# Capped attention and a top-1 expert layer in one kernel: two row steps, an eviction and a rank step change places

## The chip, the cores and the metric

One core of a Trainium2 chip runs the kernel. The time is device microseconds of one execution; the kernel before took 529.63 us, the median of three runs (528.35 to 530.30). Smaller is better. TensorE (PE) multiplies and transposes, VectorE (DVE), ScalarE (ACT) and GpSimd (POOL) work element by element, and SyncE (SP) issues most of the DMAs, one after the other in the order of its queue.

## What is computed

Attention over 4 batches, 12 heads, 448 positions of 64, with a tanh cap on the scores; its output is the input of a mixture of 8 experts, each token going to the one expert with the largest logit.

```python
scores = cap * np.tanh(scale * np.matmul(q, k.transpose(0, 1, 3, 2)) / cap)
attn = np.exp(scores - scores.max(-1, keepdims=True))
attn = attn / (attn.sum(-1, keepdims=True) + 1e-09)
x = np.matmul(attn, v).transpose(0, 2, 1, 3).reshape(1792, 768)
logits = x @ w_gate                      # 8 experts
e_idx = np.argmax(logits, axis=1)
gate_w = softmax(logits)[arange, e_idx]
eom = sigmoid(x @ w_output_gate)         # 8 columns
h = np.maximum(x[mask] @ w1[e], 0.0)     # for each expert e; mask = (e_idx == e)
out[mask] = gate_w[mask, None] * eom[mask, e, None] * (h @ w2[e])
```

## The kernel before

Attention runs in 24 units: unit u is one pair of heads of one batch, six units to a batch (batches 0 to 3). In unit u TensorE forms four blocks of scores (`qk(u, 0..3)`), ScalarE takes tanh and exp of each, and TensorE multiplies the exponentials of unit u - 1 with V (`pv(u - 1, ...)`) into one PSUM bank. `u_evac(u - 1)` (L335) then copies that bank to an SBUF tile `ut` of seven buffers: from unit 18 on ScalarE does it, except for unit 22; VectorE does it for the others. `presum(u, ...)` adds up the exponentials for the denominators, on GpSimd up to unit 21 and on VectorE for units 22 and 23. `prep(u + 2)` turns and splits K and Q of the unit after the next (tiles tk, tq).

Around these the program hangs small steps in numbered slots, by hand. Slot x of the table `at` (L507) of batch 2 is met in unit 19 + x // 4, at the place x % 4 of that unit: 0 ahead of the first pv matmuls, 1 behind them, 2 behind the third block of scores, 2.5 behind `u_evac`, 3 at the end. A batch's steps are the gate matmuls and logits, `choose` (the expert of each token), `rank_mm` and `place` (the token's place within its expert), `enter` (which scatters index and weight of each token to the tables `tab` in DRAM, four GpSimd DMAs), and six row steps `rws[0..5]`: `row_tr` (L478) turns the ut of one pair by four transposes into PSUM (tile trow), `row_out` (L485) scales it on VectorE (tile xr, four buffers) and sends it to the rows `xs` in DRAM, on SyncE's queue, for batch 3 on GpSimd's. In attention trow shares the two PSUM buffers of tag "t" with tk, tq and the rank's tile trk. `RWP` (L53) holds the slots of rows 1 to 5, row 0 has its own; `NXP` puts the six steps of `early()` into slot 7: small VectorE operations that plan the first five blocks of tokens and write the plan, `meta`. Slot 10.5 puts on SyncE's queue the table fetches of the first two blocks (`fetch_dma`, tc<-tab, four DMAs each, whose addresses come from meta) and the first weight chunk; slots 15 and 16 put the first two `gather` on GpSimd's queue and the other weight chunks on SyncE's. `gather(i)` reads the tokens' rows from xs (batches 0 to 2) into xg, and so waits for all their rows.

The experts follow: blocks of 128 tokens, each weight chunk split by ScalarE (high part) and VectorE (low part) into planes, up to six ahead, then matmuls in two sweeps (`mm1`, `mm2`). The first two blocks share their planes (`two1`, `two2`). The steps of batch 3 are the list `bg`, which `STEPS` (L58) spells out: one word to a step, one letter to a part (r rank_mm, p place, q positions, e enter, a digit a row step, n the next part of the later plan `late()`). The first two steps stand ahead of `two1`, the next twelve behind its twelve chunks, two behind the last chunks of block 2, the rest in `two2`. There a row is turned into the tile of tag "hph", which has one buffer.

Of the kernel before, what the change touches and what calls it, by code (L numbers as in the profile page):

```python
# [21 lines left out]
def tile_kernel(ctx: ExitStack, tc, q, k, v, cap, w_gate, w_ogate, w1, w2, out):  # L22
    nc = tc.nc
    B, H, S, D = q.shape
# [5 lines left out]
    NU = B * NP  # L30
# [19 lines left out]
        COL.update({k: NW + i * NO + j for j, k in enumerate(k for k in OWN if KIND[k] == kind)})  # L50
    AH = 6
    PZ = 4
    RWP = (9, 10, 12, 13, 14)  # L53
    NXP = (7, 7, 7, 7, 7, 7)
    F1 = 5
    F2 = 4
    PRE = 3
    STEPS = 'g s S G x0 X1 l2 c rp3 n4 n5 q e n n n n n n zh'  # L58
    WARM = (32, 8, 12, 0)
    RB = 7  # L60
    SP0 = 3
# [2 lines left out]
    UACT = 18  # L64
# [269 lines left out]

    def u_evac(u):  # L335
        t = utp.tile([128, S], F32, tag="ut", name="ut")
        if UACT <= u < NU - 2 or u == NU - 1:
            nc.scalar.activation(out=t, in_=ups.pop(u), func=ACTF.Copy)  # L338
        else:
            nc.vector.tensor_copy(out=t, in_=ups.pop(u))  # L340
        ut[u] = t
# [22 lines left out]
    def end_of_batch(b):  # L364
# [130 lines left out]
        rws = [L(P(row_tr, p), P(row_out, p)) for p in range(NP)]  # L495
        t = [sums_out, L(sums_tr, recips), L(P(gate_mm, 0), P(gate_out, 0)), L(P(gate_mm, 1), P(gate_out, 1))]
        gts = [L(P(gate_tr, g), P(gate_mul, g)) for g in range(2)]
        if b < B - 2:
            at = {1: [t[2], t[3]], 2: [sums_out], 5: [t[1]], 6: [rws[0]], 9: [gts[0]], 10: [rws[1]], 13: [gts[1]], 14: [rws[2]],
                  15: [logits], 16: [choose], 18: [rws[3]], 21: [rank_mm, place], 22: [rws[4]], 23: [place2], 24: [enter]}  # L500
            at.setdefault(26 if b < B - 3 else 22, []).append(rws[5])
        elif b == B - 2:
            g = early()
            nx = P(next, g, None)
            lds = [P(load_raw, 0, w, c) for w in range(2) for c in range((KD, KF)[w])]
            fd = [P(fetch_dma, i) for i in range(NE)]
            at = {-1: [sums_out], 1: [t[2], t[3]], 2: [t[1], *gts], 3: [logits], 4: [choose],  # L507
                  6: [rws[0]], 6.5: [rank_mm, place, place2, enter]}
            for i, x in enumerate(RWP, 1):
                at.setdefault(x, []).append(rws[i])  # L510
            for i, x in enumerate(NXP):
                at.setdefault(x, []).append(nx)
            for x, fs in ((10.5, [fd[0], fd[1], P(set_known, NE), lds[0]]), (15, [P(gather, 0), *lds[1:6], fd[2]]),
                          (16, [P(gather, 1), fd[3], *lds[6:]])):
                at.setdefault(x, []).extend(fs)
        if b < B - 1:
            for x, fs in at.items():
                for f in fs:
# [4 lines left out]
                  e=enter, n=nx, z=L(P(set_known, NSLOT), P(fetch_dma, NE)), h=lambda: next(rests(), None))  # L523
        do.update({str(p): rws[p] for p in range(NP)})
        return [L(*[do[x] for x in w]) for w in STEPS.split()]

# [60 lines left out]
    def early():  # L587


        cnt, key, srt, gt = M("cnt", [1, E]), M("key", [1, E]), M("srt", [1, E]), M("le", [1, E, E])  # L590
        cm, nb, nbp, more = M("cm", [1, E]), M("nb", [1, E]), M("nbp", [1, E]), M("more", [1, E])
        g14 = M("g14", [1, E, 14])
        lo, hi = M("lo", [1, 1, E]), M("hi", [1, 1, E])
        tt(cnt, pres[(B - 1) % 2][0:1, 0], ereg, ALU.subtract)

        stt(srt, cnt, float(E), ALU.mult, e8, ALU.subtract)
        ts(cm, cnt, -127.0, ALU.add)
        tt(gt, over(srt, E), srt.unsqueeze(2).to_broadcast([1, E, E]), ALU.is_gt)
        tt(g14, cm.unsqueeze(2).to_broadcast([1, E, 14]), mrow.unsqueeze(1).to_broadcast([1, E, 14]), ALU.is_gt)
        red(key, gt)  # L600
        red(nb, g14)
        yield

        ts(nbp, key, 0.0, ALU.is_equal, 2.0, ALU.mult)
        ts(more, key, float(E - 1), ALU.is_equal, float(NE), ALU.mult)
        tt(nbp, nbp, nb, ALU.max)
        tt(gt, over(key, E), key.unsqueeze(2).to_broadcast([1, E, E]), ALU.is_le)
        tt(nbp, nbp, more, ALU.add)
        yield
        tt(gt, gt, over(nbp, E), ALU.mult)  # L610
        red(hi[:, 0], gt)
        tt(lo[:, 0], hi[:, 0], nbp, ALU.subtract)
        yield
        yield from slots_of(lo, hi, nb, ereg.unsqueeze(1), 0, NE)
# [60 lines left out]
    def rests():  # L675

        full, h, hx, wo = rt["rest"]
        sh = [1, 2, NO, E]
        oh, o2 = M("roh", sh), M("ro2", sh)
        two = lambda x: x.unsqueeze(2).to_broadcast(sh)  # L680
        own = lambda i: metah[:, i, NW:].rearrange("a (z n) -> a z n", z=2)
        tt(wo, wo, over(full, NW), ALU.mult)
        tt(oh, two(hx), irow[:, 0:NO].unsqueeze(1).unsqueeze(3).to_broadcast(sh), ALU.is_equal)
        red(metah[:, 2, 0:NW], wo, ALU.max)
        tt(oh, oh, two(h), ALU.mult)
        tt(o2, oh, full.unsqueeze(1).unsqueeze(1).to_broadcast(sh), ALU.mult)
        red(own(1), oh, ALU.max)
        red(own(2), o2, ALU.max)
        tt(o2, oh, e8.unsqueeze(1).unsqueeze(1).to_broadcast(sh), ALU.mult)
        red(own(0), o2, ALU.max)  # L690
        yield
# [134 lines left out]
    for b in range(B - 1):  # L826
        end_of_batch(b)
# [32 lines left out]
    for u in range(NU):  # L860
# [24 lines left out]
        if u > 0:  # L885
            pv(u - 1, 3)
            u_evac(u - 1)
# [8 lines left out]
    u = NU - 1  # L896
# [245 lines left out]

    split_to(SP0)
    bg.extend(end_of_batch(B - 1))
    pv(u, NK)
    u_evac(u)
    tx(0)
    step()
# [96 lines left out]
```

## Time and profile before

| | |
|---|---|
| runs | 528.35, 529.63, 530.30 us |
| profiled execution | 529.51 us, of which the span is 527.9 us |
| busy: TensorE, VectorE, ScalarE, GpSimd | 97%, 65%, 73%, 56% of the span |
| mean granted clock of TensorE | 0.992 |

The span runs from the first to the last instruction; the remainder of the time lies around it. The shares are means over very unlike stretches: attention up to about 211 us, the experts from about 217 us. A wait counts for the end only where TensorE, or what follows it, has nothing else to do.

### The profile page before, as it was taken

The numbers are of one execution on the slowest core, as the hardware profiler recorded it, in microseconds if no ns is written. First come the engines' busy times: TensorE is split into PE (matmuls) and PEld (weight loads), VectorE is DVE, ScalarE is ACT, GpSimd is POOL, SyncE is SP. The second block draws the span as 40 slices with busy tenths as digits, with TensorE's granted clock in tenths as the row PEclk, the third lists the DMA queues.
The fourth block names the chain that finished last, engine by engine and source line by source line (L and its number), as shares of the span: only waits on it lengthen the run. The fifth ranks groups of instructions, "written<-read, shape, count | busy, mean of one in ns | idle before, by whom it ended". The sixth has DMA issues, their size and how long they took to land. (4 is left out here: it accounts for less than half of the span.)

```text
span 527.9 us, 10345 instructions
## 1 busy us (share of the span) xinstructions
PE 509.8 (97%) x3197; PEld 362.9 (69%) x3197; DVE 345.3 (65%) x576; ACT 382.9 (73%) x498; POOL 294.3 (56%) x341
## 2 busy tenths in 40 slices
PE   8999999999999999699999999999999999999995
PEld 7555465555655544367999898897878968666692
DVE  3263354965596867489888986885758686545460
ACT  5989897889787978435678896886767687555561
POOL 8998967778987686435245856313737025272001
PEclk9999999999999999799999999999999999999999
DMA  7544434446455317887149626329749959994001
GB/s 162 128 108 100 104 74 105 104 106 120 96 114 125 73 35 195 292 279 214 66 169 394 252 64 218 121 84 358 273 156 390 406 199 378 349 317 156 1 30 49
DMA packets 106189, 91.94 MB, mean 174 GB/s; under 512 B 80770, under 2 KB 88970, under 8 KB 106128
## 3 DMA queue, kind: packets, MB, share of 16 engines
q1 hardware_dynamic: 97088, 58.45, 38.5%
q0 software_dynamic: 8736, 32.74, 17.1%
q8 instruction: 27, 0.44, 0.3%
q14 instruction: 34, 0.28, 0.2%
q10 hardware_dynamic: 304, 0.03, 0.0%
HBM read 123.68 MB, written 12.04 MB: 257 GB/s over the span
## 5 line engine op out<-in xcount | busy, mean ns | idle before, releaser
L947 DVE TENSOR_TENSOR wr<-raw,wr 128x768 fp32r<-128x768 f32 (+1 forms) x167 | 172.0, 1067 | 68.8 <-ACT wr L946 67.9
L946 ACT ACTIVATE wr<-raw 128x768 fp32r<-128x768 f32 (+1 forms) x167 | 150.5, 935 | 32.8 <-DMA raw<-in_moe_w_dram 9.7
L302 ACT ACTIVATE th<-s,icap 128x896 f32<-128x896 f32 x96 | 84.4, 914 | 26.4 <-PE s L297 19.9
L284 ACT ACTIVATE pt<-th,capc 128x896 f32<-128x896 f32 x96 | 85.7, 946 | 0.0
L968 PE MATMUL py<-wr,hh 128*128 128x384 f32 x352 | 77.3, 340 | 0.0
L968 PE MATMUL php<-wr,xh 128*128 128x512 f32 x264 | 75.0, 405 | 0.0
L1037 POOL DMA_INDIRECT out_dram<-yo,ti x13 | 20.8, 1596 | 91.4 <-ACT yo L1035 67.3
L968 PEld LDWEIGHTS py<-wr,hh 128*128 128x128 f32 x352 | 61.2, 188 | 4.0 <-issue 3.7
L317 PE MATMUL u<-pt,vv 128*64 128x448 f32 x288 | 59.4, 548 | 0.5 <-ACT ut L338 0.5
L968 PEld LDWEIGHTS php<-wr,xh 128*128 128x128 f32 x264 | 47.7, 189 | 12.9 <-issue 2.1
L329 POOL TENSOR_TENSOR pb<-pa,pt 128x896 f32<-128x896 f32 x22 | 46.5, 2113 | 16.8 <-issue 12.5
L333 POOL TENSOR_TENSOR pb<-pb,pt 64x448 f32<-64x448 f32 x44 | 51.8, 1178 | 4.1 <-DMA tab<-ent,posi 0.8
L328 POOL TENSOR_TENSOR pa<-pt 128x896 f32<-128x896 f32 x22 | 46.3, 2104 | 2.9 <-ACT ex L439 0.8
L968 PE MATMUL py<-wr,hl 128*128 128x384 f32 x176 | 44.8, 335 | 0.0
L968 PE MATMUL php<-wr,xl 128*128 128x512 f32 x132 | 41.5, 395 | 0.0
L317 PEld LDWEIGHTS u<-pt,vv 128*64 128x64 f32 x288 | 18.5, 136 | 30.5 <-issue 22.8
L1084 POOL DMA_DIRECT2D rh<-in_moe_w_dram x42 | 23.5, 561 | 21.7 <-issue 15.7
L297 PE MATMUL s<-QH,KH 64*128 64x448 f32 x144 | 31.7, 432 | 0.9 <-ACT th L302 0.9
L968 PEld LDWEIGHTS py<-wr,hl 128*128 128x128 f32 x176 | 31.8, 188 | 0.0
L340 DVE COPY ut<-u 128x448 f32<-128x448 f32 x19 | 11.8, 622 | 29.6 <-PE u L320 29.4
L968 PEld LDWEIGHTS php<-wr,xl 128*128 128x128 f32 x132 | 24.7, 187 | 6.0
L1138 POOL DMA_INDIRECT out_dram<-yh,toh x6 | 6.2, 1033 | 37.3 <-issue 14.4
(243 smaller groups left out, 858.5 us busy)
## 6 DMA issues: line engine op xcount, KB each, us to landing
raw<-in_moe_w_dram SPq DMA_DIRECT2D x78, 512.0 KB
raw<-in_moe_w_dram SPq DMA_DIRECT2D x104, 384.0 KB
rh<-in_moe_w_dram POOLq DMA_DIRECT2D x18, 512.0 KB, 7.2
rh<-in_moe_w_dram POOLq DMA_DIRECT2D x24, 384.0 KB, 8.4
lq<-in_q_dram SPq DMA_DIRECT2D x24, 224.0 KB
kk<-in_k_dram SPq DMA_DIRECT2D x24, 192.0 KB
vv<-in_v_dram SPq DMA_DIRECT2D x24, 192.0 KB
xs<-xr SPq DMA_DIRECT2D x18, 224.0 KB
```

What stands on the lines that cost most here:

```text
L284: nc.scalar.activation(out=dst, in_=th, func=ACTF.Exp, scale=capc)
L297: nc.tensor.matmul(ps[:, j, 0:S], lhsT=x[h, sl], rhs=y[h], start=(i == 0), stop=(i == 2))
L302: nc.scalar.activation(out=th[:, 0:n], in_=ps[:, 0:n, 0:S], func=ACTF.Tanh, scale=icap)
L317: nc.tensor.matmul(ups[u][64 * j:64 * j + 64], lhsT=V[:, c, j, :], rhs=P[:, 2 * c + j], start=(c == 0), stop=False)
L328: eng.tensor_tensor(out=a, in0=P[:, 0:2], in1=P[:, 2:4], op=ALU.add)
L329: eng.tensor_tensor(out=s1[u], in0=a, in1=P[:, 4:6], op=ALU.add)
L333: eng.tensor_tensor(out=s1[u][h, j], in0=s1[u][h, j], in1=P[h, 2 * NK], op=ALU.add)
L946: nc.scalar.activation(out=t[:, 0, 0:F], in_=raw, func=ACTF.Copy)
L947: nc.vector.tensor_tensor(out=t[:, 1, 0:F], in0=raw, in1=t[:, 0, 0:F].bitcast(F32), op=ALU.subtract)
L968: nc.tensor.matmul(ps[g][:, 0:n], lhsT=st[:, c], rhs=w[:, z, g * n:(g + 1) * n], start=(c == 0 and st is hi and z == 0), stop=(c == (KD, K ...
L1037: nc.gpsimd.indirect_dma_start(out=out, out_offset=bass.IndirectOffsetOnAxis(ap=ti, axis=0), in_=y, in_offset=None, bounds_check=NT - 1, o ...
L1084: nc.gpsimd.dma_start(out=d, in_=src[bass.ds(e, 1)].rearrange("e (k p) f -> p (e k) f", p=128)[:, c], **kw)
```

## The change

Row 0 of batch 2 goes from slot 6 to 5, row 1 from 9 to 6, row 2 from 10 to 12, row 3 from 12 to 13; rows 4 and 5 stay. The ut of unit 21 is copied by VectorE and not by ScalarE. In batch 3, row 3 goes ahead of rank_mm; place goes from that step to the next one, ahead of row 4; the plan's first part of these goes from row 4's step to row 5's; q and e come one step later, and two of the plan's parts share a step, so that the list keeps its twenty steps and the plan its end.

```diff
-    RWP = (9, 10, 12, 13, 14)
+    RWP = (6, 12, 13, 13, 14)
...
-    STEPS = 'g s S G x0 X1 l2 c rp3 n4 n5 q e n n n n n n zh'
+    STEPS = 'g s S G x0 X1 l2 c 3r p4 n5 n q e nn n n n n zh'
...
     def u_evac(u):
         t = utp.tile([128, S], F32, tag="ut", name="ut")
-        if UACT <= u < NU - 2 or u == NU - 1:
+        if UACT <= u < NU - 3 or u == NU - 1:
...
             at = {-1: [sums_out], 1: [t[2], t[3]], 2: [t[1], *gts], 3: [logits], 4: [choose],
-                  6: [rws[0]], 6.5: [rank_mm, place, place2, enter]}
+                  5: [rws[0]], 6.5: [rank_mm, place, place2, enter]}
```

## Rows read from the trace of the kernel before

**Rows 1.** Busy time by stretch: PE, PEld, DVE, ACT, POOL, then clock, DMA share, GB/s

```profile
211.50:215.20 3.70, 0.01 (x1) 0.00 (x0) 3.30 (x4) 1.73 (x3) 2.82 (x4) 1.00 1.02 416
215.20:216.70 1.50, 0.00 (x0) 0.00 (x0) 0.00 (x0) 0.00 (x0) 0.00 (x0) 0.51 1.12 300
216.70:222.00 5.30, 5.24 (x24) 2.29 (x25) 1.02 (x2) 1.85 (x4) 2.36 (x7) 0.50 0.63 198
...
250.00:500.00 250.00, 250.00 (x1586) 204.06 (x1585) 180.47 (x229) 177.98 (x238) 105.82 (x143) 1.00 0.63 230
```

**Rows 2.** TensorE's waits, 170 to 252 us: for whom, total us, times, longest

```profile
PE pt_x L760 <- DMA xg<-xs,ti: 5.2, 1, 5.2
PE tk L271 <- DVE xr L487: 1.6, 2, 1.2
PE trow L483 <- DVE bcm L542: 0.7, 1, 0.7
PE u L317 <- ACT ut L338: 0.5, 1, 0.5
...
PE trk L437 <- DVE ohb L430: 0.3, 1, 0.3
```

**Rows 3.** Timeline of GpSimd, 160 to 270 us: start, us, instruction, idle before

```profile
188.66 2.10 POOL L328 TENSOR_TENSOR pa<-pt 128x896 f32<-128x896 f32 x1
...
204.47 0.75 POOL L741 TENSOR_SCALAR ti<-tb 128x1 uint32<-128x1 f32 x1
209.95 1.14 POOL L748 DMA_INDIRECT xg<-xs,ti  x1 [4.73 <-DMA raw<-in_moe_w_dram]
```

**Rows 4.** Timeline of SyncE's queue, 160 to 290 us

```profile
191.53 1.28 SPq L490 DMA_DIRECT2D xs<-xr  x2
194.55 4.90 SPq L733 DMA_DIRECT2D tc<-tab  x8
200.57 0.35 SPq L710 DMA_DIRECT2D raw<-in_moe_w_dram  x1
...
203.17 1.98 SPq L490 DMA_DIRECT2D xs<-xr  x3
...
266.69 2.05 SPq L733 DMA_DIRECT2D tc<-tab  x4
```

**Rows 5.** Timeline of VectorE, 187 to 192 us: the end of the early plan

```profile
188.46 0.14 DVE L535 TENSOR_TENSOR bch<-meta 1x4 f32<-1x4 int32 x1
...
188.74 2.04 DVE L535 TENSOR_TENSOR meta<-bch,bsm 1x4 int32<-1x4 f32 x1
...
190.84 1.27 DVE L487 TENSOR_TENSOR xr<-trow,rec 112x512 f32<-112x512 f32 x2
```

**Rows 6.** A stretch with full DMA engines, and the page's row DMAs

```profile
203.00:208.00 5.00, 5.00 (x31) 1.94 (x26) 3.46 (x8) 4.39 (x6) 1.98 (x4) 1.00 1.03 246
...
xs<-xr SPq DMA_DIRECT2D x18, 224.0 KB
```

**Rows 7.** Timeline of VectorE, 195 to 250 us: two row evictions

```profile
199.17 0.69 DVE L487 TENSOR_TENSOR xr<-trow,rec 112x512 f32<-112x512 f32 x1 [0.69 <-PE trow L483]
...
239.30 0.68 DVE L487 TENSOR_TENSOR xr<-trow,rec 112x512 f32<-112x512 f32 x1
```

**Rows 8.** Line 340, VectorE's copies of ut: ns min/median/max

```profile
L340 DVE COPY ut<-u x19: 605/625/625, 20.1 to 208.2; 128x448 f32<-128x448 f32 x19
```

**Rows 9.** Timeline of TensorE: the same work at either clock

```profile
204.84 0.96 PE L352 MATMUL sm<-pb,ohc 128*32 128x448 f32 x8
...
216.76 1.51 PE L760 MATMUL pt_x<-ident,xg 128*128 128x128 f32 x6 [5.25 <-DMA xg<-xs,ti]
...
219.70 1.72 PE L352 MATMUL sm<-pb,ohc 128*32 128x448 f32 x8
...
225.97 0.87 PE L760 MATMUL pt_x<-ident,xg 128*128 128x128 f32 x6
```

## Prediction, made before the changed kernel ran

> **What bounds the kernel now.** I read the stretches first, then TensorE's waits, then the queues behind the one long wait. From 250 to 500 us TensorE has no idle time at all [rows 1]: an experts' stage that starts x us sooner should end x us sooner, as far as the trace shows. What is left to win lies ahead of it, and the list of waits from 170 to 252 us has nearly all of it: 5.2 us for the first gather of tokens (xg), 1.6 us for VectorE's eviction of rows before the transposes of K (tk), 0.5 for ScalarE's eviction of the ut of unit 21, and in the first expert pair 0.7 and 0.3 us, before the turned row of a pair (trow) and the rank (trk) [rows 2]. The 5.2 us stand between attention and experts; in them the granted clock falls, and the first 5.3 us of work after them run at 0.50, which is 1.2 of 2.4 GHz [rows 1].
>
> So whatever ends attention sooner is worth nothing unless the gather comes sooner too. Its chain runs backwards like this. GpSimd has the first token indices ready at 205.22 (204.47 + 0.75), but issues the gather at 209.95 after 4.73 us of waiting [rows 3]. The profile puts that down to a weight load; the gather needs all rows of the first three batches in xs, the last of which SyncE issued only at 203.17 to 205.15 [rows 4], and semaphores are shared, so I read it as the last row. Those three rows stood in SyncE's queue behind eight table fetches (from 194.55), a weight chunk (200.57) and the V load of unit 23. The fetches in turn stood behind the rows of pairs 1 and 2 (191.53, 1.28 us) [rows 4], which waited for VectorE: it evicted those two at 190.84, after the early plan's small operations, whose last but one, the meta multiply, took 2.04 us from 188.74 [rows 5].
>
> **The change part by part.**
>
> *Rows 0 and 1 sooner.* Row 0 goes from slot 6 to 5, row 1 from 9 to 6; both now stand ahead of rank, place and early plan on VectorE, and ahead of the V load of unit 22 on SyncE. Removed: the two row DMAs just ahead of the fetches. Moved: one more eviction, 0.64 us (1.27 / 2) [rows 5], now lies ahead of the early plan. The plan's writes to meta ended at 190.78; with 0.64 more they end at 191.4. Before, SyncE was done with the rows at 192.81 and issued its first fetch 1.74 us later (register loads) [rows 4]. The trace has no case where SyncE waits for the plan alone. If all of the 1.74 us is still to pay, the fetch starts at 193.1, 1.4 us sooner; if only half of it, at 192.3, 2.3 us sooner. I take 1.8, nearer to the row as it stands.
>
> *Rows 2 and 3 later.* Row 2 goes from slot 10 to 12 and so behind the V load of unit 23, row 3 from 12 to 13. Four rows stand now where three stood. A row costs 0.66 us of issue (1.98 / 3) [rows 4]; its 224 KB at the 246 GB/s that the DMA engines moved while they were full (share 1.03) cost 0.93 us [rows 6]. As the engines are full, I take 0.93; bounds 0.66 and 0.93. The evictions are not late: VectorE began that of the last row at 199.17 [rows 7], and SyncE would come to it at 203 at the earliest.
>
> Together the last row, the gather and TensorE's restart come 1.8 - 0.93 = 0.9 us sooner, from 0.5 (1.4 - 0.93) to 1.6 (2.3 - 0.66). GpSimd's own chain (table scatters, presums, indices) starts with the rank and moves 0.64 later, to 205.9; it had 4.73 us to spare, so it hides. Should that cover go, it costs at most those 0.64.
>
> *The 1.6 us before tk.* 1.2 of them come from rows 1 and 2 holding both buffers of the transposes while VectorE is in the early plan. They go, and row 2's and row 1's transposes leave unit 21. ScalarE is late next there: it must evict ut and copy K and Q right behind its exponentials. I give it a few tenths, and all of it falls into the wait for the gather: zero for the end.
>
> *The eviction of ut 21 by VectorE.* Removed: one copy on ScalarE behind the exponentials of unit 22, on which TensorE waited 0.5 us [rows 2]; added: one on VectorE, 0.62 us by the nineteen it does already [rows 8], between the last row and the presum of unit 22. The wait goes, also ahead of the gather: zero. What hides both is the idle 5.2 us; attention ends at about 211.3 in place of 211.5.
>
> *The last batch's steps.* Row 3 now goes ahead of the rank, place follows with row 4, the plan's next step with row 5, and q and e (positions and entries) one place later. The 0.3 us wait of the rank for the choice is filled with row 3's transposes. The 0.7 us was row 4's transposes waiting for row 3's eviction, which VectorE began at 239.30, behind place [rows 7]: rows here have one PSUM buffer. Now that eviction stands before place. By VectorE's order (split, row 3, place, row 4) each row is evicted 0.2 to 0.3 us before the next needs the buffer, so I count both waits as gone: 0.95 us, from 0.4 to 1.0. Four scatters to the tables go out one chunk later, and with them the fetch for slot 5; SyncE's next fetches of tables came only at 266.69 [rows 4], behind weight loads that wait for their buffers, so nobody should wait.
>
> **Sum.** The profiled execution took 529.51 us (527.9 of span, 1.6 around it), 0.12 under the median of 529.63. 529.51 - 0.9 - 0.95 = 527.7.
>
> **The rivals.**
>
> *The clock is kept.* In the trace it fell while TensorE stood idle, shortly before the restart (1.00 from 211.5 to 215.2, 0.51 from 215.2) [rows 1]. The wait becomes 0.7 to 0.9 us shorter. If the clock then does not fall, the first work runs at full speed: six transposes of tokens took 1.51 us there and 0.87 later at 1.00, eight matmuls of the sums 1.72 and, earlier, 0.96 [rows 9], 1.77 times as long together; 5.3 us at that rate are 3.0 at full, 2.3 less: 527.7 - 2.3 = 525.4. For it: the fall came so late in the wait. Against: the wait stays over 4 us. The Trainium skill ("TensorE: Matmul & The Clock Gate", Part 1) says that the throttled state is the default and that the point of change differs between runs of one kernel; the one trace here cannot show the second. Chance 0.25.
>
> *The lock goes the other way.* The meta multiply started 0.08 us after GpSimd's presum (188.66, 2.10 us) and ended 0.02 after it [rows 3, 5]; the same line's operation at 188.46 took 0.14. If it comes first, the early plan ends 1.9 us sooner. The table scatters, which the fetch needs, then bind; I estimate a fetch 1.3 us sooner than above: 526.4, and with the clock kept some 524. Both engines follow the same eviction, so the margin should stay. The Trainium skill ("SBUF — State Buffer", Who interferes with whom) has the rule: a VectorE instruction with two SBUF inputs and a GpSimd instruction that reads SBUF exclude each other for the whole instruction, and issue order decides who waits. The row agrees, 2.04 us. Chance 0.08.
>
> *The gather gains nothing.* The fetch starts no more than 0.9 sooner because something else that the trace hides in the 1.74 us holds it, and the fourth row eats that. Only the 0.95 us stay: 528.6. (The other half may fail instead, if VectorE holds up the first pair elsewhere: 528.6 again.) Chance 0.14.
>
> *The lock takes one more.* The plan could slip against GpSimd, so that the multiply meets the second operation of that presum and not the first; by the first it would then end 2.1 later than above, at 193.5; fetches and rows come 0.65 later than before and the fourth row adds 0.93: the gather 1.6 later, 529.51 + 1.6 - 0.95 = 530.2. It decides from a plan that ends later than 192.8 on. Against: it takes a slip of 2 us, where both engines follow one eviction. Chance 0.06.
>
> **How the numbers follow.** The forecast has 0.47 (526.8 to 528.6 by its bounds). Half a per cent is 2.6 us, about what a measurement of this kernel can tell from no change; faster by more means under 527.0. That takes the kept clock (0.25), the lock the other way (0.08) and the lower end of the forecast (0.06): 0.38 with a little off. Slower by over 0.5%, above 532.3, needs more than any rival gives: 0.03. The range from 525.0 to 529.4 leaves out the slower rival and the best of the lock.
>
> **What would show it.** Right: in the changed trace SyncE's first table fetch starts near 192.7 and four row DMAs go out in a run until about 204; the wait before the first transposes of tokens is some 4.5 us with its end near 215.9; no wait for tk at unit 21 nor for ut 21; in the first pair no wait before trow and at most 0.1 before trk. Wrong: a first fetch after 193.7, a GpSimd that reaches the first gather later than the last row, a wait for VectorE before the weight planes, or a clock that stays at 1.00 across the wait, which would put the time at 525.

## The result and the profile after

The changed kernel took 524.33 us (median of four runs, 522.71 to 525.40), against 529.49 us before (four runs, 528.35 to 530.30). The ratio is 0.9904, 95% interval 0.9886 to 0.9922: 5.1 us faster, 4.1 to 6.0. That is below the forecast (527.7) and below the low end of the range (525.0). The sign was right; the gain was 2.8 times what I had worked out.

The profiled execution took 525.11 us, of which the span is 523.4; its mean granted clock is 0.992, as before. The five waits of TensorE from 170 to 252 us (for whom, total us, times, longest), beside [rows 2]:

```profile
PE trow L483 <- DVE KL L252: 2.2, 1, 2.2
PE pt_x L760 <- DMA xg<-xs,ti: 0.7, 1, 0.7
PE s L297 <- ACT th L302: 0.6, 1, 0.6
PE tq L258 <- PE tk L271: 0.5, 1, 0.5
PE tk L271 <- DVE xr L487: 0.4, 1, 0.4
```

The 5.2 us before the first token transposes (pt_x) have become 0.7, the 1.6 before tk 0.4, and the waits for ut, for bcm and for ohb are gone. New are two waits inside attention, 2.2 us for the buffer of a row's transposes (trow), which VectorE frees only behind the split of K (KL), and 0.6 us for ScalarE's tanh. SyncE's queue, beside [rows 4] (start, duration, instruction), issues nothing between the V load that ends at 183.48 and the fetches:

```profile
179.99 1.26 SPq L490 DMA_DIRECT2D xs<-xr  x2
...
189.68 4.93 SPq L733 DMA_DIRECT2D tc<-tab  x8
...
198.32 5.87 SPq L490 DMA_DIRECT2D xs<-xr  x4
```

The table fetches begin 4.87 us sooner (194.55 to 189.68), and four rows go out in a run. Now VectorE at the plan's end, as in [rows 5], and two evictions of late rows:

```profile
188.39 0.19 DVE L532 TENSOR_REDUCE meta<-bo 1x5 int32<-1x40 f32 x1
...
188.78 2.02 DVE L535 TENSOR_TENSOR meta<-bch,bsm 1x4 int32<-1x4 f32 x1
...
201.09 1.29 DVE L487 TENSOR_TENSOR xr<-trow,rec 112x512 f32<-112x512 f32 x2 [4.78 <-PE trow L483]
```

The multiply into meta is the row that contradicts the prediction: SyncE's first fetch at 189.68 starts 1.1 us **before** the multiply ends (188.78 + 2.02 = 190.80). GpSimd's indices and first gather, as in [rows 3]:

```profile
202.79 0.23 POOL L741 TENSOR_SCALAR ti<-tb 128x1 uint32<-128x1 f32 x1
207.89 1.36 POOL L748 DMA_INDIRECT xg<-xs,ti  x1 [4.87 <-DMA xs<-xr]
```

GpSimd had the indices at 203.02 and waited 4.87 us for the last row, so the gather came 2.06 us sooner than before and not 4.87. The rows were late because TensorE was: VectorE waited 4.78 us for their transposes. Busy time by stretch (PE, PEld, DVE, ACT, POOL, clock, DMA share, GB/s), as in [rows 1]:

```profile
192.30:194.40 2.10, 0.00 (x0) 0.00 (x0) 0.66 (x2) 2.10 (x5) 1.95 (x3) 0.87 0.11 2
194.40:200.60 6.20, 6.12 (x18) 2.34 (x19) 1.25 (x3) 3.39 (x4) 5.96 (x4) 0.50 0.58 158
...
215.40:222.00 6.60, 6.59 (x42) 3.76 (x42) 5.84 (x8) 4.80 (x7) 4.57 (x6) 1.00 0.68 203
250.00:500.00 250.00, 250.00 (x1588) 204.69 (x1587) 181.88 (x234) 178.51 (x239) 104.23 (x140) 1.00 0.62 226
```

In this execution the idle time and the half clock have changed places. TensorE stood still for 2.1 us at 192.3, inside attention, and then ran 6.2 us at 0.50; but attention's end and the experts' start now follow each other with 0.7 us between them, and the experts start at a clock of 1.00. From 250 to 500 us there is again no idle time.

TensorE's first token transposes began at 215.41 in place of 216.76 [rows 9]: only 1.35 us sooner. The remainder came behind that point. TensorE's last instructions, first in the kernel before, then in this one:

```profile
516.46 5.38 PE L1108 MATMUL pyh<-raw,hth 128*64 128x384 f32 x32
```

```profile
511.71 5.38 PE L1108 MATMUL pyh<-raw,hth 128*64 128x384 f32 x32
```

They end at 521.84 and 517.09, 4.75 us apart: 1.35 from the restart, 2.3 for the 5.3 us at half clock that are no longer there (5.3 - 5.3/1.77, an estimate by the prediction's rate), and 1.0 for the two waits in the first pair, which leaves 0.1.

Two more profiles of the same kernel (e8 and e15 of the experiments below) show another division of about the same sum. There the wait inside attention is 1.0 us and not 2.2, the clock stays at 1.00 in it, the rows go out by 201.2, and the first gather waits for nothing but its own indices. One wait, then GpSimd and TensorE, in e8:

```profile
PE trow L483 <- DVE KL L252: 1.0, 1, 1.0
```

```profile
204.84 0.48 POOL L741 TENSOR_SCALAR ti<-tb 128x1 uint32<-128x1 f32 x1
205.78 1.14 POOL L748 DMA_INDIRECT xg<-xs,ti  x1 [0.46 <-POOL ti L741]
...
212.93 1.42 PE L760 MATMUL pt_x<-ident,xg 128*128 128x128 f32 x6 [2.90 <-DMA xg<-xs,ti]
```

and its stretches:

```profile
210.00:212.90 2.90, 0.03 (x1) 0.00 (x0) 2.73 (x4) 0.61 (x2) 0.46 (x1) 1.00 1.05 361
212.90:216.50 3.60, 3.57 (x18) 1.60 (x22) 2.55 (x4) 1.30 (x3) 0.78 (x4) 0.53 0.26 51
```

The restart is 3.83 us sooner than before, after a wait of 2.90, and the half clock lasts some 3.4 us of the 3.6 shown, not 5.3. By the same estimate that makes 3.83 + 0.8 for the shorter half clock + 1.0 for the two waits, 5.6; TensorE's work ends 4.94 us sooner. Of the missing 0.7, 0.4 is a wait of TensorE in the experts that neither the kernel before nor the first profile has; the other 0.3 stay open. In e15 the end is 5.78 us sooner: 3.85, 0.8 and 1.0, which leaves 0.13. So the change brings 4.75, 4.94 and 5.78 us in the three profiles, however the idle time falls.

### The profile page after: what moved, and what is told of

Read it like the earlier page. It is cut to its first block, busy times and chain, and to the rows that moved or that the text cites. A ratio compares the mean times of both kernels' runs of the same rounds, so it can differ in the third digit from the quotient of the medians.

```text
span 523.4 us, 10345 instructions
## 1 busy us (share of the span) xinstructions
PE 509.6 (97%) x3197; PEld 362.7 (69%) x3197; DVE 344.0 (66%) x577; ACT 381.8 (73%) x497; POOL 296.4 (57%) x341
## 5 line engine op out<-in xcount | busy, mean ns | idle before, releaser
L1037 POOL DMA_INDIRECT out_dram<-yo,ti x13 | 19.5, 1503 | 89.5 <-ACT yo L1035 65.0
L317 PE MATMUL u<-pt,vv 128*64 128x448 f32 x288 | 61.7, 565 | 0.0
L333 POOL TENSOR_TENSOR pb<-pb,pt 64x448 f32<-64x448 f32 x44 | 50.2, 1140 | 4.0 <-DMA tab<-ent,posi 0.7
```

The source lines that it names most:

```text
L317: nc.tensor.matmul(ups[u][64 * j:64 * j + 64], lhsT=V[:, c, j, :], rhs=P[:, 2 * c + j], start=(c == 0), stop=False)
L333: eng.tensor_tensor(out=s1[u][h, j], in0=s1[u][h, j], in1=P[h, 2 * NK], op=ALU.add)
L1037: nc.gpsimd.indirect_dma_start(out=out, out_offset=bass.IndirectOffsetOnAxis(ap=ti, axis=0), in_=y, in_offset=None, bounds_check=NT - 1, o ...
```

## Experiments

All ratios are to runs of the kernel before on the same chip, with 95% intervals.

### One part at a time

**The last batch's steps alone** (e1_steps).

```diff
-    STEPS = 'g s S G x0 X1 l2 c rp3 n4 n5 q e n n n n n n zh'
+    STEPS = 'g s S G x0 X1 l2 c 3r p4 n5 n q e nn n n n n zh'
```

> The kernel before with the new step list of the last batch alone. Theory A (the large part of the gain comes from SyncE's queue: no row that waits for VectorE stands ahead of the table fetches, so the first gather and TensorE's restart come sooner and the clock need not fall in the wait): this part gives only its two waits in the first expert pair, 0.95 us, so about 528.5. Theory B (the gain comes from attention ending sooner): the same 528.5. Theory C (the step list is the main part): about 525.

Measured: 528.17 us, ratio 0.9977 (0.9967 to 0.9988), so 1.2 us faster (0.6 to 1.7). TensorE's waits from 170 to 252 us in its profile:

```profile
PE pt_x L760 <- DMA xg<-xs,ti: 4.8, 1, 4.8
PE tk L271 <- DVE xr L487: 1.7, 2, 1.3
PE u L317 <- ACT ut L338: 0.5, 1, 0.5
PE tq L258 <- PE tk L271: 0.5, 1, 0.5
PE trow L483 <- DVE KL L252: 0.2, 1, 0.2
```

The waits for bcm (0.7) and ohb (0.3) of [rows 2] are the two that are missing, all others stand. The 0.95 of the prediction lies within the interval.

**The rows alone** (e2_rows).

```diff
-    RWP = (9, 10, 12, 13, 14)
+    RWP = (6, 12, 13, 13, 14)
...
-                  6: [rws[0]], 6.5: [rank_mm, place, place2, enter]}
+                  5: [rws[0]], 6.5: [rank_mm, place, place2, enter]}
```

> The kernel before with the four moved rows alone (slots 5, 6, 12, 13). Theory A: nearly all of the gain but the step list's, so about 525.3, with the first table fetch on SyncE near 189.7 us of the span and not 194.6, since it waits only for the part of the plan that it reads (written at about 188.6) and not for the plan's end at 190.8. Theory B: a part, about 527, the rest with the eviction. Theory C: about 528.7.

Measured: 525.46 us, ratio 0.9930 (0.9910 to 0.9950), 3.7 us faster. SyncE's fetches in its profile:

```profile
189.57 4.87 SPq L733 DMA_DIRECT2D tc<-tab  x8
```

Most of what the prediction missed lies in this part, for which it had 0.9.

**The eviction alone** (e3_evac).

```diff
-        if UACT <= u < NU - 2 or u == NU - 1:
+        if UACT <= u < NU - 3 or u == NU - 1:
```

> The kernel before with the copy of ut 21 on VectorE alone. Theory A: no change, 529.5 within 0.5, because what it saves falls into the wait for the first gather. Theory B: a gain of 0.5 to 1, about 528.8. In either case no wait of TensorE for that copy in the trace.

Measured: 528.85 us, ratio 0.9998 (0.9986 to 1.0009). By itself the eviction is worth nothing that shows, as forecast (0.6 us slower to 0.7 faster would be within the interval). In its profile the wait for ut is gone, and the wait for the gather is 5.1 us, no longer than before; where the 0.5 us went isn't shown. The three parts add up to 1.2 + 3.7 + 0.1 = 5.0 us, against 5.1 for the whole: no interaction is seen, though the intervals leave room for one of 1 us.

### What in the rows does it

**Row 2 back ahead of the fetches** (e4_row2_back), the changed kernel with one row's DMA where it was before:

```diff
-    RWP = (6, 12, 13, 13, 14)
+    RWP = (6, 10, 13, 13, 14)
```

> The changed kernel with row 2 put back to slot 10, where VectorE evicts it only behind the plan. Theory A: its DMA stands ahead of the table fetches on SyncE again and waits for VectorE until about 191.5 us, so the first fetch starts near 193 to 194, the last row and the gather come about as in the kernel before or up to 1.5 sooner (one row less ahead of them than before), and most of the gain is lost: 527 to 528.5. Theory B: row 2 holds one transpose buffer over the plan, which costs TensorE a few tenths at most: 524.3 to 525.

Measured: 527.61 us, ratio 0.9968 (0.9957 to 0.9979). One row back gives away 0.64% of 529 us, some 3.4 us. SyncE's queue:

```profile
191.53 0.59 SPq L490 DMA_DIRECT2D xs<-xr  x1
193.70 4.88 SPq L733 DMA_DIRECT2D tc<-tab  x8
...
202.29 2.00 SPq L490 DMA_DIRECT2D xs<-xr  x3
```

The fetches are back at 193.70, and the wait for the gather is 5.7 us. What is left of the gain is that of the steps (1.2 of 1.7), within the intervals.

**The two rows on another queue** (e10_rows_pool): the kernel before, every instruction of every engine in its old slot, but GpSimd issues the DMAs of rows 1 and 2 of batch 2.

```diff
-            (nc.gpsimd if b == B - 1 else nc.sync).dma_start(
+            (nc.gpsimd if b == B - 1 or (b == B - 2 and p in (1, 2)) else nc.sync).dma_start(
```

> The kernel before, its slots unchanged, with the DMAs of rows 1 and 2 of batch 2 issued by GpSimd and not by SyncE. Nothing is moved on TensorE, VectorE or ScalarE. Theory A (SyncE's queue): the first table fetch starts near 189.7 us with the plan still unfinished, the remaining three rows go out right behind the V load, and most of the gain is there: 525 to 527, less what the two DMAs cost GpSimd's queue of presums (about 1.4 us, which the first indices may have to spare). Theory B (transposes and evictions moved): no gain, 529 or more.

Measured: 525.76 us, ratio 0.9929 (0.9902 to 0.9955), 3.8 us faster: as much as the whole part of the rows. SyncE's queue, then VectorE's multiply, then GpSimd:

```profile
188.94 4.82 SPq L733 DMA_DIRECT2D tc<-tab  x8
```

```profile
188.04 2.04 DVE L535 TENSOR_TENSOR meta<-bch,bsm 1x4 int32<-1x4 f32 x1
```

```profile
194.62 1.47 POOL L490 DMA_DIRECT2D xs<-xr  x2
...
206.57 1.81 POOL L748 DMA_INDIRECT xg<-xs,ti  x1 [0.42 <-POOL ti L741]
```

The fetches start 1.1 us before the multiply ends here too (188.04 + 2.04 = 190.08). Neither VectorE's order nor the transposes were touched, so it is shown that the two row DMAs in SyncE's queue were what held the fetches, and that the fetches did not need the multiply. The rows themselves went out only at 194.62, and the gather waits for its own indices and not for them. The two DMAs had a price on GpSimd: its indices are ready at 206.15, 0.9 us later than before [rows 3].

### What the clock is worth

**The wait filled, in the kernel before** (e6_before_busy): 48 multiplications of a constant into an unused PSUM tile (keep) stand in TensorE's queue between attention and the first token transposes. All of the kernel's own work stays.

```diff
+    keep = ps_x.tile([128, 512], F32, tag="hph", name="keep")
+    for _ in range(48):
+        nc.tensor.matmul(keep[:, 0:128], lhsT=onesb, rhs=onesb, start=True, stop=True)
```

> The kernel before with 48 small bf16 matmuls on a constant, into an unused PSUM tile, between the end of attention and the first transposes of tokens: TensorE is busy for the larger part of the wait for the first gather. It measures the clock's share by itself. If the fall of the clock in that wait costs what rows of either clock say (2.3 us), and the matmuls keep it up: 526.7, with the gather at the same place. If the clock falls anyway: 529 to 530.

Measured: 527.52 us, ratio 0.9959 (0.9935 to 0.9982), 2.2 us faster with more work. Its stretches, and the wait for the gather that is left:

```profile
213.40:216.30 2.90, 2.82 (x48) 2.66 (x47) 1.19 (x2) 0.03 (x1) 2.49 (x4) 1.00 0.94 330
216.80:222.00 5.20, 5.18 (x36) 3.35 (x37) 2.04 (x3) 3.96 (x7) 2.39 (x8) 1.00 0.85 266
```

```profile
PE pt_x L760 <- DMA xg<-xs,ti: 0.5, 1, 0.5
```

The token transposes start when they did before (216.82 against 216.76), and the work after them runs at 1.00 in place of 0.50. The gain is 1.0 to 3.4 us by the interval, and the 2.3 us at which the rival put the half clock lie within it.

**The same in the changed kernel** (e7_after_busy), same edit.

> The changed kernel with the 48 small matmuls on a constant between attention and the first transposes of tokens. In one of its two profiles the clock fell in the wait for the first gather, in the other it had fallen before and was back. If the changed kernel pays for that fall in most executions, this gives up to 1.6 us: 522.7. If it mostly keeps its clock: 524.3, and no more than 0.5 lost when the gather is early.

Measured: 526.20 us, ratio 0.9945 (0.9924 to 0.9965), slower than the changed kernel (0.9904) by some 2 us. In its profile the 48 start 0.63 us behind attention, after ScalarE's last copy of ut, and hold the transposes until 215.20, 2.3 us later than in e8:

```profile
212.52 2.84 PE L1149 MATMUL keep<-onesb 112*128 112x128 bf16 x48 [0.63 <-ACT ut L338]
```

With 2.9 us or less of wait left, the filler is longer than the wait. What the slower runs pay is not seen, though: the profiled execution is one of the two fastest, 524.80 us, and its TensorE ends when that of e8 does (516.86 and 516.90). The four runs of 525.98 to 527.66 us have no profile.

### What bounds the gather now

**The changed kernel again** (e8_after_again, e15_after3), for its profile and as the reference of the runs beside it.

> The changed kernel once more, for a second profile and for the runs to compare with. 524.3. Open from the first profile: TensorE's results of unit 21 reach ScalarE 1.9 us late, the row's transposes of unit 22 then hold TensorE idle for 2.2 us, and the clock falls there, at 194 us. If that is a matter of one execution, this profile has no such wait, and the gather comes 2 us sooner or more; if it belongs to the order, it is here again.

> The changed kernel again, beside the two others on the same chip: 524.3.

Measured: 524.31 us, ratio 0.9895 (0.9855 to 0.9934), and 524.05 us, ratio 0.9901 (0.9880 to 0.9922). Their profiles are the second and third of the section on the result: the gather went out at 205.78 and 205.66, bound by GpSimd's own chain, and TensorE restarted at 212.93 and 212.91.

**GpSimd relieved of a presum** (e11_presum21_vec), and **with the filler** (e12_both).

```diff
-        eng = nc.vector if u >= NU - 2 else nc.gpsimd
+        eng = nc.vector if u >= NU - 3 else nc.gpsimd
```

> The changed kernel with the presum of unit 21 on VectorE and not on GpSimd. In its second profile the first gather waited for GpSimd's own chain (indices ready at 205.3 us) and no longer for the rows, issued by 201.2. If GpSimd is the new bound of the gather: indices near 198, the gather issued at the last row's landing near 204.5 to 205, TensorE back 1 us sooner, 523.3. If the rows or the DMA engines are the bound: 524.3; if VectorE's added 3.5 us push the rows' evictions back by 2 us or more: 525 or over.

> The changed kernel with both: presum of unit 21 on VectorE and the 48 matmuls in the wait. If both causes hold: 521.7 to 522.5. If neither does: 524.3 or a little over.

Measured: 524.27 us, ratio 0.9908 (0.9891 to 0.9925), so no gain on the changed kernel, and 526.77 us, ratio 0.9960 (0.9946 to 0.9975). GpSimd's rows in e11, and a row eviction:

```profile
197.90 0.61 POOL L741 TENSOR_SCALAR ti<-tb 128x1 uint32<-128x1 f32 x1
208.31 1.27 POOL L748 DMA_INDIRECT xg<-xs,ti  x1 [9.80 <-DMA xs<-xr]
```

```profile
201.42 1.29 DVE L487 TENSOR_TENSOR xr<-trow,rec 112x512 f32<-112x512 f32 x2 [1.65 <-PE trow L483]
```

The indices come 4.9 us sooner than in the first profile of after and then wait 9.80 us for the last row. This is not VectorE's doing: e11's profile fell as the first one did, with the wait of 2.2 us in attention and the half clock behind it, and the late evictions wait for TensorE's transposes (201.42 here, 201.09 there). So it doesn't tell what the presum costs where the indices bind the gather. Two profiles without that half clock do, e7 and e12, which differ in the presum alone; their gathers, e7 first:

```profile
205.58 1.14 POOL L748 DMA_INDIRECT xg<-xs,ti  x1 [0.39 <-POOL ti L741]
```

```profile
206.50 1.40 POOL L748 DMA_INDIRECT xg<-xs,ti  x1 [8.33 <-DMA xs<-xr]
```

With the presum on VectorE, TensorE waits another 1.4 us for an eviction before a row's transposes, the rows are out at 202.85 and not at 201.41, and the gather goes out 0.9 us later, bound by the last row. In this pair moving work from GpSimd to VectorE loses what it frees.

**Row 2 one slot later still** (e9_row2_13).

```diff
-    RWP = (6, 12, 13, 13, 14)
+    RWP = (6, 13, 13, 14, 14)
```

> The changed kernel with row 2 at slot 13 and rows 4 and 5 at 14: no row's transposes stand ahead of the pv matmuls of unit 22, so TensorE does not sit behind a transpose buffer that VectorE frees only after the K and Q of unit 23. Theory A (the last row's landing sets the restart, and in the changed kernel that row is late because TensorE idles 2.2 us there and then works at half clock): the rows go out at 198 to 201 us in place of 198 to 204, the gather comes 2 to 3 us sooner, about 521.5. If the wait for the gather is set by the DMA engines and not by the rows: 524.

Measured: 526.00 us, ratio 0.9920 (0.9892 to 0.9947): not the gain expected, and no better than the changed kernel (524.31 beside it). The gather went out at 206.19 without waiting for a row, but TensorE saw its tokens only 8.0 us later:

```profile
206.19 1.84 POOL L748 DMA_INDIRECT xg<-xs,ti  x1 [0.34 <-POOL ti L741]
```

```profile
214.23 0.97 PE L760 MATMUL pt_x<-ident,xg 128*128 128x128 f32 x6 [3.50 <-DMA xg<-xs,ti]
```

**Three weight chunks behind the gather** (e13_raw_pool, e16_raw_pool2: the same kernel), **and with row 2 at 13** (e14_both): the first block's chunks 3 to 5 are issued by GpSimd, behind its first gather, and not by SyncE ahead of it.

```diff
-            ... (15, [P(gather, 0), *lds[1:6], fd[2]]),
+            ... (15, [P(gather, 0), *lds[1:3], *[P(load_raw, 0, 0, c, nc.gpsimd) for c in range(3, 6)], fd[2]]),
```

> The changed kernel with weight chunks 3 to 5 of the first block issued by GpSimd behind the first gather, and not by SyncE ahead of it. In all kernels so far the first gather landed 6.3 to 8 us after its issue, with five chunks of 512 KB issued just ahead of it, and 16 to 18 us after the first chunk's issue. If the DMA engines' backlog of those chunks sets the landing: 1.5 MB less ahead, the wait from issue to TensorE's restart shrinks to some 4.5 to 5 us, the restart comes at about 210.5, bounded by the end of attention, the clock need not fall: 522. If the time from issue to landing is the gather's own: 524.3, or 525 with GpSimd's second gather 2.5 us later.

> The changed kernel with chunks 3 to 5 behind the gather again, for a comparison on one chip: 523.6, under the changed kernel by 0.5 to 1.5; if the wait for the gather is really gone in most executions, by more than 1.

> The changed kernel with weight chunks 3 to 5 behind the first gather and row 2 at slot 13 (rows 4 and 5 at 14). If the DMA backlog bounded the gather where row 2 alone was moved, and the end of attention bounds it where the chunks alone were moved, both together gain the 2.2 us that TensorE stood behind the transpose buffer: 521.5 to 522, with attention ending near 209.5 to 210.5 us. If the backlog is not what made row 2 at 13 slower, this is slower than the chunks alone again, by 1 us or more.

Measured: 523.60 us, ratio 0.9901 (0.9881 to 0.9920); 523.73 us, ratio 0.9899 (0.9877 to 0.9921); and 523.44 us, ratio 0.9880 (0.9861 to 0.9899). In e13 the gather's data are there when attention ends (lines stand 2 lower in this kernel):

```profile
205.29 1.14 POOL L750 DMA_INDIRECT xg<-xs,ti  x1 [0.39 <-POOL ti L743]
206.68 1.73 POOL L712 DMA_DIRECT2D raw<-in_moe_w_dram  x3 [0.26 <-issue]
```

```profile
210.59 1.02 PE L320 MATMUL u<-pt,vv 128*128 128x448 f32 x2
211.44 0.82 PE L762 MATMUL pt_x<-ident,xg 128*128 128x128 f32 x6
```

The wait is gone, the clock stays at 1.00 from 203 to 222 us, and the restart is 1.5 us sooner than in e8 and e15. Yet e16 and e14 are only 0.3 and 0.6 us below the changed kernel beside them (e15), and the intervals overlap; e13, whose profiled execution was its fastest (521.91), has none beside it. In e16's profile the second block pays:

```profile
205.95 1.14 POOL L750 DMA_INDIRECT xg<-xs,ti  x1 [0.46 <-POOL ti L743]
```

```profile
210.28 0.88 PE L762 MATMUL pt_x<-ident,xg 128*128 128x128 f32 x6
...
220.27 0.85 PE L762 MATMUL pt_x<-ident,xg 128*128 128x128 f32 x6 [1.62 <-DMA xg<-xs,ti]
```

In e16 the gather's data are there 4.33 us after its issue at the latest; with five chunks ahead it took 7.15 us in e8 and 7.25 in e15. So the chunks just ahead of the gather do hold up its landing. They are not all of it: in e10 TensorE still waited when the DMA engines' share had fallen to 0.19:

```profile
211.00:212.90 1.90, 0.04 (x2) 0.04 (x1) 1.84 (x3) 0.61 (x2) 1.58 (x3) 1.00 0.19 34
```

The gain seems to be given back where the second block's tokens (1.62 us in e16) and VectorE's split (waits of 0.45 to 0.93 us before php) come due; no run takes these waits away, so that is argued and not shown. No version here is shown to beat the changed kernel.

## Why the prediction was right or wrong

**The step that failed** is the first term, "Rows 0 and 1 sooner". It let the first fetch wait for the end of the plan's writes to meta, 191.4, and so forecast a start at 192.7, 1.8 us sooner. It started at 189.68, 4.87 us sooner. I had taken the multiply of 2.02 us for a writer that SyncE waits for, because it writes meta and the fetches read addresses from meta. But the fetches read only `meta[:, 2, i]`, which the reduction at 188.39 had written by 188.58; the multiply writes `meta[:, 1, ...]`. In after and in e10 the fetch starts 1.1 us after that reduction and 1.1 us before the multiply ends. That it needs no multiply is shown. What it does wait for is not separated: GpSimd's last table scatter is issued within 0.1 us of the reduction's end in both (188.64 and 187.91), and the fetches read those tables. In the kernel before, only the two row DMAs, waiting for VectorE's evictions behind the multiply, carried the multiply's 2 us onto SyncE's queue. I had written that the trace has no case of SyncE waiting for the plan alone, and bounded the cost from the end of the wrong instruction. The bound (1.4 to 2.3) left out the case that the fetch doesn't need the last writer.

**A small error beside it:** the plan was to end 0.64 us later for the additional eviction ahead of it. It did not: the multiply started at 188.78 against 188.74 [rows 5].

**From 4.87 to the restart.** Of the fetches' 4.87 us the restart got 1.35 in one profile and 3.83 and 3.85 in the others. The prediction had the fourth row's 0.93 as the only loss, and GpSimd's chain covered by 4.73 us. In the two profiles the rows are out 4 us sooner (201.19 in e8, 205.15 before), the cover is used up, and the indices, as late as ever (ready at 205.32 in e8, 205.22 before [rows 3]), release the gather. In the first profile something else held the rows. The wait before tk came back in front of the row transposes in slot 12: VectorE's split of K, which frees their buffer, waited for ScalarE's copy of K, and TensorE stood still for 2.2 us. The prediction had ScalarE next in line there, but gave it a few tenths and nothing for the end. The reading that the gather waits for the last row, against the name in [rows 3], is borne out there: the profile names xs<-xr. The prediction named a GpSimd that reaches the first gather later than the last row as a sign of its being wrong.

**The clock.** The forecast had it unchanged; the rival "the clock is kept" had 0.25 and 525.4 us, which is near the measured time by luck: it kept a wait of over 4 us, and no profile of after has one. In the first profile the clock fell inside attention, in the wait of 2.2 us, and was back at 1.00 from 200.7 us on; in the other two it fell behind the restart and was half for some 3.4 us. The rival's price, 2.3 us, stands (e6: 2.2). The Trainium skill ("TensorE: Matmul & The Clock Gate", Part 1) says that the point of change differs between runs of one kernel. The second and third profiles agree: after waits of 2.90 and 2.99 us the clock fell at about 213.1 and 214.4, 0.2 and 1.5 us behind the restart.

**The steps of the last batch:** 0.95 forecast, 1.2 measured alone (0.6 to 1.7), both waits gone. Right within the interval.

**The wait before tk and the eviction:** tk's wait fell from 1.6 to 0.4, ut's vanished, and e3 shows the eviction at zero within 0.7 us, as forecast. Right as far as that; the wait of 2.2 or 1.0 us that took tk's place was not forecast.

**The lock:** in every profile of the runs above the multiply meets GpSimd's presum and takes 2.02 to 2.05 us, so neither lock rival happened. The Trainium skill ("SBUF — State Buffer", Who interferes with whom) describes such a lock, and the rows agree; what the change altered is who stands behind it.

**The sum** would have come out near with the right first term: 4.87 - 0.93 + 0.95 = 4.9, against 5.1 measured. That is partly luck. The restart's 3.83 and 3.85 us in e8 and e15 lie near 4.87 - 0.93, but there GpSimd's indices bound it and not the fourth row, and the clock gave 0.8 more; in the first profile the restart gave 1.35 and the clock 2.3.

## What to carry to other kernels

Where a queue issues in order, look at the head: a DMA that waits for a slow engine delays all that stands behind it, and moving it behind them, or to another queue (e10, 3.8 us for one edited line), frees them; see what the move costs where it goes. When you forecast what such a transfer waits for next, ask which instruction writes the elements that it reads, not which one last wrote that tile. And look one bound further: here GpSimd's chain, the DMA backlog and the second block's tokens each came up as a wait of 0.9 to 3.5 us in some profile, and no later edit is shown to gain.

## What the runs showed of the hardware

- A fetch whose address comes from a small tile started 1.1 us before a later instruction, which writes other elements of that tile, had ended (189.68 against 190.80; e10: 188.94 against 190.08).
- A gather issued behind five weight chunks was used, as soon as it was there, 6.3 us (e10) to 8.0 us (e9) after its issue; with three of those chunks behind it, it was there within 4.33 us in e16 (205.95 to 210.28) and after 5.27 us in e14.
- Filling a wait of 5.2 us with 2.84 us of work on a constant kept TensorE's clock at 1.00 for the first 5.2 us behind it, which had run at 0.50, and gained 2.2 us of 529 (e6). The same work in a wait of 2.9 us or less lost some 2 us (e7).
- Not settled: in some profiles ScalarE began a tanh of unit 21's scores about 2 us later than in others. Its idle time before it is 2.83 us in the first profile of after, 0.94 in the second. The long one (2.83) stands in e1 as well, whose attention is that of the kernel before, so the change doesn't cause it; what does, no run here tells. Nor does a run tell why the clock falls in the wait of 2.2 us that follows it in three profiles (after, e2, e11) and not in three others (e7, e12, e13).

The first of these two rows is from the first profile of after, the second from e8:

```profile
189.76 1.53 ACT L302 ACTIVATE th<-s,icap 128x896 f32<-128x896 f32 x2 [2.83 <-PE tk L271]
```

```profile
188.08 1.53 ACT L302 ACTIVATE th<-s,icap 128x896 f32<-128x896 f32 x2 [0.94 <-PE s L297]
```

Also open is why e9 is not faster than the changed kernel although its rows go out as early: its gather took 8.04 us to its use, against 7.15 in e8. The weight loads ahead of it would explain some of that, and with them moved (e14) the same order gives the lowest median of all, 523.44, but not by more than the intervals allow.
